# Block 0 of a fused attention and two-MLP kernel in another order: first weights fetched first, memory values copied by GpSimd, three value chunks sent from ScalarE

## The chip, the cores and the metric

The kernel runs on one core of a Trainium2 chip. The metric is the device time of one execution in microseconds (us), the median of three runs. Engines are named as in the profile: PE (TensorE matmul), PEld (its weight load), DVE (VectorE), ACT (ScalarE), POOL (GpSimd) and SP (SyncE, which here only issues DMAs).

## What is computed

Chunked attention with eight memory keys and values, then two MLPs one after the other, all in float32. The reference, cut:

```python
def _attn_ref(q, k, v, mem_k, mem_v):      # q, k, v: (4, 8, 768, 64); mem: (4, 8, 8, 64)
    for c in range(S // 32):               # chunks of 32 queries
        k_ctx = k[:, :, max(0, 32 * c - 16):min(S, 32 * c + 40)]        # v_ctx the same
        k_full, v_full = concat(mem_k, k_ctx), concat(mem_v, v_ctx)
        scores = scale * (q_c @ k_full.T)
        a = exp(scores - max(scores)); a = a / (sum(a) + 1e-09)
        out[:, :, 32 * c:32 * c + 32] = a @ v_full

def _moe_ref(x, w1, w2, w3, w_out):        # x: 3072 tokens x 512, d_ff 768
    return maximum(maximum(x @ w1, x @ w2), x @ w3) @ w_out

def _moe2_ref(x, w_in, w_out):             # d_ff 2048
    h = x @ w_in
    g = where(h >= 1, h, where(h <= -1, 0, (h + 1) ** 2 / 4))
    return g @ w_out
```

## The kernel before, in words

The 3072 tokens are worked in blocks of 512 (six blocks) and units of 128 (24 units, four to a block). A float32 product is made of three fast products: each operand is split into a high and a low part, and PE does high x high, high x low and low x high (L499, L500, L501). So every weight and every activation has to be split by ACT (high part) and DVE or GpSimd (low part) before PE may use it.

Block 0 is the start of the program: no weight is split yet and no attention is done. Its order is written out as a table of names, `PLAN`; each name is one step of one unit or weight, and every engine gets its instructions in the order of the table. Engines wait for each other by semaphores alone, so on each engine a step that waits holds up all that stands behind it in that engine's row. From the end of the table on, loops set the order, and they are the same in both kernels.

The steps, by their names in the table (the number is the unit, the weight or the slot):

- `d`: four matmuls on the identity matrix whose result nobody reads (`warm`, L1011); they keep PE at work.
- `lk`, `lq`: fetch a unit's keys or queries (256 KB, from SP). `lmem`, `mem`: fetch and transpose the memory keys (copied out of PSUM on DVE at L1002). `lm`: fetch the memory values of a batch (`mv`, 16 KB).
- `lv`: fetch a unit's values into its window buffer (`vw`, `vxh` or `vxl`): four chunks of 32 queries, two DMAs each, eight DMAs from SP (L265). `mv`: spread the eight memory values into the four chunks of that buffer, two DMAs from SP (L254).
- `tk`, `ck`, `ek`, `kw`, `tq`, `cq`: transposes on PE and copies on ACT that lay out keys and queries.
- `s`: the scores, 64 small matmuls (L378). `mx` on DVE: maximum and subtraction (L392, L393). `ex` on ACT: exponential (L397). `n` on DVE: sum, 1e-9, reciprocal, multiplication (L401 to L404). `a`, `ca`: transpose the probabilities (L410) and copy them. `o`: times the values (L426). `cx` on ACT: high part of the unit's activations (L436); `dx` on DVE: their low part (L440).
- `f`: fetch one weight (512 KB, L121 or L119); two weights make a pair, which lies in one of two staging buffers (`st`). A pair is split in six steps: `wa` (absolute value, ACT L134), `wr` (tail, ACT L138), `wc` (three bit operations, DVE L142, L143, L145), `wd` (their sum, DVE L150), `wh` (high part, ACT L199), `ws` (low part, DVE L204). Pair 0 holds the first two weights of the first layer, pair 1 the third one and the first of the second layer.
- `l`: a slot of the first layer, twelve matmuls of 512 columns; l0, l1 take pair 0, l2 pair 1, l3, l4 pair 2, and so on. `lt`: copy (ACT) or maximum (DVE, L534). `lh`: split of the hidden activations. `m`: a slot of the second layer.

The first slot, l0, takes the activations of units 0 to 3 and pair 0, so it stands behind `dx3` and `ws0`. `ON_DVE` and `ON_POOL` say which copies and low parts leave their usual engine; before, nothing of block 0 is on GpSimd but four memsets and the identity matrix.

Of the kernel before, what the change touches and what calls it, by code (L numbers as in the profile page):

```python
# [41 lines left out]
mv0 mx0 lq2 tk2 mv1 ck2 ek2 lk4 tq1 ex0 lv0 cq1 n0 tk3 kw1 ck3 s1 ek3 a0 kw2 mx1 tq2 lq3 tk4 cq2 f0
ck4 f1 s2 ex1 lk5 f2 d3 ek4 mx2 f3 kw3 lq4 lv2 ca0 n1 tq3 ex2 o0 cq3 n2 a1 cx0 s3 ca1 dx0 wa0 mx3 o1
wr0 tk5 wc0 a2 cx1 d7 d7 ca2 d7 ex3 d7 dx1 ck5 d7 d7 ek5 wd0 kw4 n3 wa1 tq4 f4 cq4 lv3 wc1 wr1 s4
wh0 o2 kw5 wd1 a3 d7 cx2 d7 ws0 f5 wh1 d7 lq5 f6 dx2 ca3 f7 mx4 lk7 o3 lv4 ws1 ex4 d7 cx3 d7 n4 wa2
tq5 wr2 dx3 a4 wc2 cq5 ca4 s5 l0 wa3 wd2 wr3 mx5 f9 l1 f8 wh2 lv5 wc3 ex5 lt0 o4 n5 l2 cx4 lt1 ws2
lq7 a5 lq6 wd3 ca5 l3 lm1 wa4 dx4 lk6 f11 lt2 wr4 f10 wc4 l4 lh2 lt3 wh3 wd4 tq7 o5 cq7 ws3 f13 wh4
f12 tk6 mv6 l5 cx5 ws4 lk8 ck6 lv6 dx5 wa5 lt4 tq6 lt5 wr5 m0 wc5 cq6 lh5 wa6 l6 wd5 wr6 wc6 lq8 f14
wh5 f15 tk7 l7 lt6 lk9 ck7 ws5 ek7 kw6 wd6 l8 lt7 f16 wh6 f17 ws6 s6 lt8 wa7 m1 mx6 wr7 wc7 lh8 ex6
tq8 l9 cq8 wa8 wd7 m2 wr8 wc8 f18 f19 lt9 wh7 l10 wd8 ws7 f21 wh8 f20 n6 tk8 l11 ck8 ek8 lt10 kw7  # L50
# [9 lines left out]
-  # L60
# [1129 lines left out]
```

## Time and profile before

| | |
|---|---|
| median of 3 runs | 963.79 us (961.11 to 964.07) |
| profiled execution | 960.31 us |
| its span, first to last instruction | 958.5 us |
| mean granted TensorE clock | 0.996 |
| PE busy | 938.7 us (98%) |
| DVE busy | 704.6 us (74%) |
| ACT busy | 541.9 us (57%) |
| GpSimd busy | 339.6 us (35%) |

Durations come from the profiled execution, which was 3.5 us faster than the median. The share of a whole span hides its stages, so the views that matter here are those cut to the first 125 us: the table of busy time by stretch, the timelines of single engines, and the waits.

### The profile page before, as it was taken

What the parts mean: (1) busy time and instruction counts of PE and PEld (TensorE: products, weight loads), DVE (VectorE), ACT (ScalarE), POOL (GpSimd) and SP (SyncE); (2) the same over time, 40 slices, a digit from 0 to 9 for tenths busy, and PEclk for the clock granted to TensorE, in tenths of its full rate; (3) what the DMA queues carried; (4) which work ended last, traced back from release to release, by engine and by line L of the source; (5) the groups of instructions that cost most, each with busy time, mean ns of one, the idle gap of its engine ahead of it and who ended that gap; (6) DMA issues with size and microseconds to landing.
All of it is one profiled execution on the core that took longest, in us unless ns stands there. A gap on an engine that the chain in (4) does not pass through costs nothing.

```text
span 958.5 us, 18892 instructions
## 1 busy us (share of the span) xinstructions
PE 938.7 (98%) x7090; PEld 772.4 (81%) x7090; DVE 704.6 (74%) x1001; ACT 541.9 (57%) x972; POOL 339.6 (35%) x330
## 2 busy tenths in 40 slices
PE   6799999999999999999999999999999999999998
PEld 5588887888888888888888888888888888888886
DVE  3999857687877777753337778997777988777855
ACT  5767554333343324223447777776777776777763
POOL 0000003221321111111746555555565555655642
PEclk8999999999999999999999999999999999999999
DMA  7896635676657677343414229524326744232823
GB/s 180 233 228 204 181 111 158 167 214 198 198 157 202 170 190 238 107 136 110 134 58 136 80 81 306 168 34 110 93 84 199 221 119 95 88 94 85 261 66 67
DMA packets 245900, 142.81 MB, mean 149 GB/s; under 512 B 174513, under 2 KB 223537, under 8 KB 245809
## 3 DMA queue, kind: packets, MB, share of 16 engines
q1 hardware_dynamic: 245808, 141.60, 51.9%
q8 instruction: 56, 0.92, 0.4%
q14 instruction: 36, 0.29, 0.1%
HBM read 109.71 MB, written 31.46 MB: 147 GB/s over the span
## 4 chain that ended last, share of the span: by engine, by line
PE 93%; DVE 4%; SPq 1%; DMA 1%; ACT 1%; issue 0%; POOL 0%; DVEq 0%; POOLq 0%
PE psums L499 29%; PE psums L501 29%; PE psums L500 29%; PE psums L426 2%; PE psums L378 2%; PE psums L410 1%; DMA kq<-in_k_dram 1%; PE psums L273 1%; DVE c L150 0%; PE psums L1011 0%; DVE p L404 0%; DVE p L393 0%; DVE few L392 0%; PE psums L304 0%; SPq L360 0%
## 5 line engine op out<-in xcount | busy, mean ns | idle before, releaser
L518 POOL TENSOR_TENSOR hl_a<-t,hh_a 128x512 fp32r<-128x512 f32 x30 | 41.5, 1383 | 384.6 <-ACT hh_a L516 384.6
L499 PE MATMUL psums<-xh,hi 128*128 128x512 f32 x432 | 172.2, 399 | 0.0
L501 PE MATMUL psums<-xh,lo 128*128 128x512 f32 x432 | 168.7, 390 | 0.0
L500 PE MATMUL psums<-xl,hi 128*128 128x512 f32 x432 | 168.2, 389 | 0.2 <-DVE xl L440 0.2
L810 POOL TENSOR_TENSOR hb<-h,hb 128x512 fp32r<-128x512 f32 x72 | 99.8, 1386 | 92.2 <-PE psums L501 59.5
L802 ACT CAST hb<-h 128x512 fp32r<-128x512 f32 x144 | 88.8, 622 | 48.1 <-PE psums L500 45.9
L534 DVE TENSOR_TENSOR t<-psums,t 128x512 f32<-128x512 f32 x72 | 49.4, 686 | 66.7 <-PE psums L501 66.7
L629 POOL TENSOR_TENSOR hb<-ra,hb 128x256 fp32r<-128x256 f32 x96 | 75.2, 796 | 58.8 <-ACT hb L628 53.8
L501 PEld LDWEIGHTS psums<-xh,lo 128*128 128x128 f32 x432 | 81.1, 188 | 17.8 <-DVE lo L204 0.3
L499 PEld LDWEIGHTS psums<-xh,hi 128*128 128x128 f32 x432 | 81.1, 188 | 16.5
L500 PEld LDWEIGHTS psums<-xl,hi 128*128 128x128 f32 x432 | 81.2, 188 | 16.4 <-DVE xl L440 0.6
L694 ACT ACTIVATE psums<-h 128x512 f32<-128x512 f32 x96 | 57.9, 603 | 60.0 <-DVE h L780 23.6
L501 PE MATMUL psums<-t,hb 128*128 128x512 f32 x192 | 74.8, 390 | 0.0
L499 PE MATMUL psums<-t,hb 128*128 128x512 f32 x192 | 74.7, 389 | 0.0
L500 PE MATMUL psums<-t,hb 128*128 128x512 f32 x192 | 74.7, 389 | 0.0
L629 POOL TENSOR_TENSOR hb<-rb,hb 128x256 fp32r<-128x256 f32 x72 | 55.5, 778 | 39.5 <-ACT hb L628 39.5
L808 DVE TENSOR_TENSOR hb<-psums,hb 128x512 fp32r<-128x512 f32 x66 | 44.9, 680 | 24.8 <-PE psums L501 20.3
L695 ACT ACTIVATE psums<-psums 128x512 f32<-128x512 f32 x96 | 55.9, 582 | 3.1
L499 PE MATMUL psums<-hh_a,hi 128*128 128x512 f32 x144 | 57.5, 399 | 0.0
L835 DVE TENSOR_TENSOR h<-h,h 128x1024 f32<-128x1024 f32 (+1 forms) x42 | 56.5, 1367 | 0.0
L501 PE MATMUL psums<-hh_a,lo 128*128 128x512 f32 x144 | 56.2, 390 | 0.0
L500 PE MATMUL psums<-hl_a,hi 128*128 128x512 f32 x144 | 56.2, 390 | 0.0
(145 smaller groups left out, 2235.9 us busy)
## 6 DMA issues: line engine op xcount, KB each, us to landing
ra<-cd SPq DMA_DIRECT2D x24, 512.0 KB
st<-in_moe_w_out_dram SPq DMA_DIRECT2D x22, 512.0 KB
t<-sd SPq DMA_DIRECT2D x21, 512.0 KB
st<-in_moe_w_dram SPq DMA_DIRECT2D x18, 512.0 KB
vw<-in_v_dram SPq DMA_DIRECT2D x152, 56.0 KB
st<-in_moe_w_in_dram SPq DMA_DIRECT2D x16, 512.0 KB
sd<-st SPq DMA_DIRECT2D x8, 896.0 KB
h<-yd SPq DMA_DIRECT2D x12, 512.0 KB
```

What stands on the lines that cost most here:

```text
L499: nc.tensor.matmul(out, whi, xhi, start=first, stop=False)
L500: nc.tensor.matmul(out, whi, xlo, start=False, stop=False)
L501: nc.tensor.matmul(out, wlo, xhi, start=False, stop=last)
L518: e.tensor_tensor(out=lo, in0=h, in1=hi.bitcast(F32), op=ALU.subtract)
L534: nc.vector.tensor_tensor(out=cur["t", j, f], in0=s, in1=cur["t", j, f], op=ALU.max)
L629: nc.gpsimd.tensor_tensor(out=c[:, 1], in0=t, in1=c[:, 0].bitcast(F32), op=ALU.subtract)
L694: nc.scalar.activation(out=a, in_=x, func=AF.Relu, bias=0.5, scale=0.5)
L695: nc.scalar.activation(out=a, in_=a, func=AF.Square)
L802: nc.scalar.copy(out=hi, in_=x)
L808: nc.vector.tensor_tensor(out=lo, in0=y, in1=hi.bitcast(F32), op=ALU.subtract)
L810: nc.gpsimd.tensor_tensor(out=lo, in0=x, in1=hi.bitcast(F32), op=ALU.subtract)
L835: nc.vector.tensor_tensor(out=x, in0=y, in1=z, op=op)
```

## The change

`PLAN` is another order of the same steps: the same slots, units and weights, and the same split of each weight. Three kinds of steps are new. `vs` and `vc` are one chunk of a unit's values, two DMAs each, sent from SP and from ACT (number = 4 x unit + chunk); they take the place of `lv0` to `lv7`, and three chunks, 6, 10 and 18, go through ACT. `mv0` to `mv2` are on GpSimd: two copies of 8 partitions x 1024 words each in the place of two DMAs. `mv6` stays a DMA. There are 16 `d` steps ahead of l0 where there were 18, and two more behind the last slot, m5. Of the table, the diff shows the first and the last line:

```diff
 PLAN = """
-d3 lk1 d3 lmem0 d3 d3 lk0 d3 lm0 lq0 lv1 tk1 mem0 ck1 tk0 ck0 ek1 tq0 lk2 kw0 d3 mv2 cq0 lq1 lk3 s0
...
-lq9 l16 lt15 wd11 m4 n7 wh11 ws11 a7 lt16 l17 ca7 o7 lt17 lh17 s8 cx7 dx7 m5 mx8 ex8 f24 f25 f26 f27
+d7 f0 d7 d7 d3 f1 lmem0 d7 d3 lk0 wa0 d3 lk1 wr0 tk0 wc0 ck0 tk1 wd0 mem0 ck1 ek1 d7 f3 d3 wh0 d7
...
+d7 d7 f24 f25 f26 f27
 """.split()
...
 ON_POOL = """
--
+mv0 mv1 mv2
 """.split()
 
 
@@ -248,21 +250,33 @@
                     out=mvs[b][e * 64:e * 64 + NM],
                     in_=mem_v[b].rearrange("(e h) m d -> e m h d", e=2)[e])
 
+    def load_vs(x):
+        load_v(x // NC, (x % NC,))
+
+    def load_vc(x):
+        load_v(x // NC, (x % NC,), nc.scalar)
+
     def fill_mv(u):
         mv = mvs[u // UPB]
+        if f"mv{u}" in ON_POOL:
+            for e in range(2):
+                nc.gpsimd.tensor_copy(
+                    out=vws[u][e * 64:e * 64 + NM].rearrange("p c h d -> p c (h d)"),
+                    in_=mv[e * 64:e * 64 + NM].rearrange("p (o g) d -> p o (g d)", o=1).to_broadcast([NM, NC, 4 * D]))
+            return
         for e in range(2):
             nc.sync.dma_start(
                 out=vws[u][e * 64:e * 64 + NM],
                 in_=mv[e * 64:e * 64 + NM].rearrange("p (o g) d -> p o (g d)", o=1).to_broadcast([NM, NC, 4 * D]))
 
-    def load_v(u):
+    def load_v(u, chunks=range(NC), queue=nc.sync):
         b, s0 = divmod(u, UPB)
-        for c in range(NC):
+        for c in chunks:
             t0 = s0 * P + c * CH - LEFT
             lo, hi = max(t0, 0), min(t0 + WIN, S)
             for e in range(2):
                 p0 = e * 64 + NM + lo - t0
-                nc.sync.dma_start(
+                queue.dma_start(
                     out=vws[u][p0:p0 + hi - lo, c],
                     in_=v[b].rearrange("(e h) t d -> e t h d", e=2)[e, lo:hi])
 
@@ -440,7 +454,7 @@
         nc.vector.tensor_tensor(out=lo, in0=t, in1=hi.bitcast(F32), op=ALU.subtract)
 
     parts = {
-        "lk": load_k, "lq": load_q, "lv": load_v, "lm": load_mv, "mv": fill_mv,
+        "vs": load_vs, "vc": load_vc, "lk": load_k, "lq": load_q, "lv": load_v, "lm": load_mv, "mv": fill_mv,
         "tk": st_k, "ck": cp_k, "ek": edge_k, "kw": fill_kw,
         "tq": st_q, "cq": cp_q,
         "s": st_s, "mx": st_m, "ex": st_e, "n": st_n, "a": st_a, "ca": cp_a, "o": st_o, "cx": cp_x, "dx": cp_xl,
@@ -484,7 +498,7 @@
         if kind in ("gk", "gq"):
             if i < NU // (3 if kind == "gk" else 2):
                 parts[kind](i)
-        elif kind in WEIGHTS or i < NU:
+        elif kind in WEIGHTS or i < (NU * NC if kind in ("vs", "vc") else NU):
             parts[kind](i)
 
     todo = [s for u in range(UB, NU) for s in steps(u)]
```

In the built program DVE's row began with the memory keys and the first unit's softmax:

```order
L992 MEMSET vw 32x256
L993 MEMSET vw 32x256
L1002 COPY memkT<-psums 64x32 x8
L384 MEMSET psums 32x2x4x16
L392 TENSOR_REDUCE few<-psums 128x8
L393 TENSOR_TENSOR p_215<-psums,few 128x512
L401 TENSOR_REDUCE few<-p_215 128x8
L402 TENSOR_SCALAR few<-few 128x8
L403 RECIPROCAL few<-few 128x8
L404 TENSOR_TENSOR p_215<-p_215,few 128x512
```

and now begins with pair 0 (c_136) and pair 1 (c_189), around the memory keys, ahead of the first unit's softmax:

```order
L1006 MEMSET vw 32x256
L1007 MEMSET vw 32x256
L144 TENSOR_SCALAR c_136<-c_136 128x1024
L145 TENSOR_SCALAR c_136<-c_136 128x1024
L147 SCALAR_TENSOR_TENSOR c_136<-st_110,c_136 128x1024
L152 ISA c_136<-st_110,c_136 128x2048
L1016 COPY memkT<-psums 64x32 x8
L206 TENSOR_TENSOR lo_181<-c_136,hi_180 128x1024
L144 TENSOR_SCALAR c_189<-c_189 128x1024
L145 TENSOR_SCALAR c_189<-c_189 128x1024
L147 SCALAR_TENSOR_TENSOR c_189<-st_174,c_189 128x1024
L398 MEMSET psums 32x2x4x16
```

Eight instructions moved to the front: all five of pair 0's and the three bit operations of pair 1. `few` and `p` are the first unit's softmax.

SP's row, the order of the fetches, began with k and memory keys, and reached the first weight behind five k (`kq<-in_k`), four q, the values of units 0 and 1 and the spread memory values:

```order
L233 DMA kq<-in_k_dram 128x8x64
L981 DMA memk<-in_mem_k_dram 128x2x64 x2
L233 DMA kq<-in_k_dram 128x8x64
L247 DMA mv_130<-in_mem_v_dram 8x4x64 x2
L239 DMA kq<-in_q_dram 128x8x64
L265 DMA vxh<-in_v_dram 56x4x64 x8
L233 DMA kq<-in_k_dram 128x8x64
L254 DMA vxl<-mv_130 8x4x256 x2
L239 DMA kq<-in_q_dram 128x8x64
L233 DMA kq<-in_k_dram 128x8x64
```

and now has the first two pairs (st_110, st_174) around the first k and the memory keys; no `mv` is spread by DMA:

```order
L123 DMA st_110<-in_moe_w_dram 128x4x256 x2
L995 DMA memk<-in_mem_k_dram 128x2x64 x2
L235 DMA kq<-in_k_dram 128x8x64 x2
L121 DMA st_174<-in_moe_w_out_dram 128x1024
L123 DMA st_174<-in_moe_w_dram 128x4x256
L241 DMA kq<-in_q_dram 128x8x64
L235 DMA kq<-in_k_dram 128x8x64
L249 DMA mv_202<-in_mem_v_dram 8x4x64 x2
L235 DMA kq<-in_k_dram 128x8x64
L241 DMA kq<-in_q_dram 128x8x64
L123 DMA st_267<-in_moe_w_dram 128x4x256 x2
L241 DMA kq<-in_q_dram 128x8x64
```

GpSimd's row goes, in the program's first part, from its memsets (kT) straight to block 1's work before:

```order
masks.py:199 AFFINE_SELECT ident<-ident 128x128
L986 MEMSET kT_82 128x4x16
L987 MEMSET kT_82 128x4x8
L518 TENSOR_TENSOR hl_a_0_1786<-t_0_1621,hh_a_0_1785 128x512
L169 TENSOR_TENSOR st_1603<-st_1603 128x512
```

and has the six copies between them now:

```order
masks.py:199 AFFINE_SELECT ident<-ident 128x128
L1000 MEMSET kT_82 128x4x16
L1001 MEMSET kT_82 128x4x8
L263 COPY vxh<-mv_202 8x1024 x2
L263 COPY vw<-mv_202 8x1024 x2
L263 COPY vxl<-mv_202 8x1024 x2
L532 TENSOR_TENSOR hl_a_0_1786<-t_0_1621,hh_a_0_1785 128x512
```

They take the place of the six DMAs from `mv` to the same three buffers in SP's row.

## Rows read from the trace of the kernel before

**Rows 1.** Stretch, length, busy PE, PEld, DVE, ACT, POOL, clock, DMA share, GB/s.

```profile
0.00:6.60 6.60, 5.24 (x25) 4.06 (x26) 0.54 (x2) 1.28 (x1) 0.85 (x8) 1.00 0.68 153
6.60:20.00 13.40, 7.98 (x162) 6.16 (x161) 5.54 (x17) 7.78 (x17) 0.00 (x0) 0.75 0.79 170
20.00:30.00 10.00, 7.65 (x282) 6.30 (x281) 7.58 (x16) 8.12 (x14) 0.00 (x0) 0.99 1.05 298
30.00:46.90 16.90, 11.39 (x319) 9.31 (x317) 16.38 (x24) 13.63 (x20) 0.00 (x0) 1.00 0.76 199
46.90:124.90 78.00, 78.00 (x784) 63.60 (x776) 71.36 (x93) 48.83 (x67) 0.00 (x0) 1.00 0.73 199
```

**Rows 2.** Timeline of PE, four places: start, us, line, operation, tiles, shape.

```profile
42.24 1.05 PE L1011 MATMUL psums<-ident 128*128 128x256 bf16 x8
...
46.93 0.50 PE L499 MATMUL psums<-xh,hi 128*128 128x512 f32 x1
...
56.56 0.60 PE L410 MATMUL psums<-ident,p 128*128 128x128 f32 x4
56.91 0.47 PE L499 MATMUL psums<-xh,hi 128*128 128x512 f32 x1
...
125.16 0.39 PE L499 MATMUL psums<-xh,hi 128*128 128x512 f32 x1
```

**Rows 3.** Waits of DVE up to 47 us: us in total, times, longest.

```profile
DVE few L392 <- PE psums L378: 5.0, 2, 3.1
```

**Rows 4.** Timeline of DVE from 33 to 46 us.

```profile
33.53 0.68 DVE L401 TENSOR_REDUCE few<-p 128x8 f32<-128x512 f32 x1
...
34.69 0.69 DVE L404 TENSOR_TENSOR p<-p,few 128x512 f32<-128x512 f32 x1
35.30 0.69 DVE L142 TENSOR_SCALAR c<-c 128x1024 f32<-128x1024 f32 x1
...
38.11 1.23 DVE L150 CUSTOM_DVE_ANT_0 c<-st,c 128x2048 uint16<-128x2048 uint16 x1
39.25 1.22 DVE L204 TENSOR_TENSOR lo<-c,hi 128x1024 fp32r<-128x1024 f32 x1
40.39 0.68 DVE L440 TENSOR_TENSOR xl<-psums,xh 128x512 fp32r<-128x512 f32 x1
40.99 0.68 DVE L392 TENSOR_REDUCE few<-psums 128x8 f32<-128x512 f32 x1
...
45.21 0.68 DVE L440 TENSOR_TENSOR xl<-psums,xh 128x512 fp32r<-128x512 f32 x1
```

**Rows 5.** Timeline of ACT: the first operation on a weight.

```profile
27.08 1.13 ACT L134 ACTIVATE c<-st 128x1024 f32<-128x1024 f32 x1 [0.27 <-DMA st<-in_moe_w_dram]
```

**Rows 6.** Timeline of SP's issues; DMA rate in 40 slices of 0 to 50 us.

```profile
25.57 7.39 SPq L265 DMA_DIRECT2D vxl<-in_v_dram  x8
...
GB/s 0 74 243 217 205 188 139 131 171 163 267 157 163 215 163 131 122 306 343 321 285 346 370 290 190 110 34 63 299 204 179 65 95 340 276 273 394 303 195 136
```

**Rows 7.** Timeline of GpSimd and DVE together in block 1, 146 to 149 us.

```profile
146.35 1.29 POOL L169 TENSOR_TENSOR st<-st 128x512 fp32r<-128x512 f32 x1 [1.93 <-ACT st L168]
...
146.60 0.68 DVE L401 TENSOR_REDUCE few<-p 128x8 f32<-128x512 f32 x1
...
147.60 1.29 POOL L169 TENSOR_TENSOR c<-c,st 128x512 fp32r<-128x512 f32 x1
...
147.94 1.50 DVE L404 TENSOR_TENSOR p<-p,few 128x512 f32<-128x512 f32 x1
```

**Rows 8.** GpSimd by line: ns min/median/max; by group: busy us, mean ns.

```profile
L518 POOL TENSOR_TENSOR hl_a<-t,hh_a x30: 1284/1302/1745, 142.8 to 494.5; 128x512 fp32r<-128x512 f32 x30
...
L629 POOL TENSOR_TENSOR hb<-ra,hb x96: 731/741/1720, 475.3 to 876.7; 128x256 fp32r<-128x256 f32 x96
...
masks.py:197 POOL MEMSET ident<- 128x128 f32 x1 | 0.2, 205 | 0.3 <-POOLq L1174 0.3
...
L987 POOL MEMSET kT<- 128x32 f32 x1 | 0.1, 126 | 0.0
```

More of the change, by code (lines that the diff above doesn't have):

```diff
@@ L40 @@
 PLAN = """
-d3 lk1 d3 lmem0 d3 d3 lk0 d3 lm0 lq0 lv1 tk1 mem0 ck1 tk0 ck0 ek1 tq0 lk2 kw0 d3 mv2 cq0 lq1 lk3 s0
[L42 to L50, printed above, removed]
@@ L51 @@
-ws8 wa9 tk9 lt11 l12 wr9 wc9 ck9 wa10 a6 lh11 wd9 l13 ek9 wr10 f22 f23 wc10 ca6 lt12 m3 wh9 wd10 o6
-ws9 wh10 s7 lt13 cx6 lv7 ws10 wa11 l14 mx7 wr11 kw8 dx6 l15 lq10 lt14 ex7 lk10 wc11 lk11 lh14 lm2
-lq9 l16 lt15 wd11 m4 n7 wh11 ws11 a7 lt16 l17 ca7 o7 lt17 lh17 s8 cx7 dx7 m5 mx8 ex8 f24 f25 f26 f27
+d7 f0 d7 d7 d3 f1 lmem0 d7 d3 lk0 wa0 d3 lk1 wr0 tk0 wc0 ck0 tk1 wd0 mem0 ck1 ek1 d7 f3 d3 wh0 d7
+ws0 f2 wa1 wc1 lq0 d7 kw0 lk2 lm0 d7 tq0 cq0 tk2 wr1 ck2 s0 lk3 ek2 kw1 mv1 lq1 mx0 tk3 f5 f4 lq2
@@ new lines @@
+tq1 vs2 ex0 cq1 vs3 lk4 ck3 s1 d3 ek3 vs1 wd1 n0 kw2 a0 wa2 tq2 mx1 d3 vs0 wr2 vc6 ex1 wc2 cq2 tk4
+mv0 n1 ca0 s2 o0 lq3 ck4 ek4 mv2 vs7 tq3 vs9 mx2 kw3 cx0 lk5 a1 vs4 vs5 lq4 wd2 vs8 cq3 ca1 ex2 s3
+tk5 vs11 vs14 dx0 mx3 wh2 vs13 lq5 vc10 n2 o1 d3 cx1 ex3 ck5 vs12 tq4 a2 ca2 vs15 dx1 f7 o2 vs19 ek5
+n3 kw4 cq4 cx2 f6 ws2 a3 s4 ca3 kw5 dx2 tq5 o3 mx4 cq5 cx3 dx3 s5 wh1 mx5 d7 f8 l0 ex4 ws1 wr3 n4
+wa3 wc3 vc18 f9 vs17 lt0 lk6 vs16 wd3 lq7 l1 lq6 wa4 wr4 lt1 l2 wc4 a4 tq7 ca4 cq7 wh3 o4 wd4 wh4
@@ new lines @@
+ws3 cx4 l3 tq6 ex5 f11 lt3 f10 lt2 tk6 wa5 ws4 vs22 vs21 ck6 n5 l4 a5 wc5 ca5 lk7 vs20 f13 lt4 cq6
+dx4 f12 l5 lh2 tk7 wr5 vs23 wr6 wd5 lt5 wa6 l6 wc6 ck7 wd6 wh5 l7 lt6 o5 lk8 lt7 ek7 kw6 tk8 ws5 lh5
+wh6 f14 lm1 cx5 f15 f16 wa7 mv6 ck8 s6 ws6 f17 vs27 dx5 ek8 mx6 vs25 l8 vs26 lm2 wc7 wr7 l9 kw7 lq8
+lk10 m0 lt8 vs24 ex6 wd7 lk9 f18 l10 wr8 wa8 f19 wh7 lt9 wc8 tk9 ck9 wd8 f21 wh8 ws7 m1 n6 wa9 tq8
+ws8 lt10 wr9 f20 wc9 lh8 lq10 a6 l11 ca6 wd9 l12 f22 lt11 cq8 o6 ek9 wa10 s7 wr10 cx6 vs30 f23 wc10
@@ L54 @@
+wd10 lt12 m2 l13 wh9 wh10 ws9 lq9 ws10 mx7 ex7 l14 vs29 lt13 n7 wa11 lt14 dx6 l15 wc11 kw8 wr11 wd11
+lk11 a7 vs31 l16 ca7 lh11 s8 vs28 wh11 ws11 mx8 lt15 lh14 o7 lt16 cx7 l17 lt17 dx7 m3 m4 ex8 lh17 m5
+d7 d7 f24 f25 f26 f27
 """.split()
```

## The prediction

> **What bounds the kernel now.** The page's first part comes first: PE is busy for 98% of the span and DVE for 74%, so over the whole program PE is the bound, and a change to block 0 can only take away time in which PE has no useful matmul. The table by stretch says where that is [rows 1]. From 46.9 to 124.9 us, PE is busy in 78.00 of 78.00 us; before 46.9 it is busy in 5.24 + 7.98 + 7.65 + 11.39 = 32.3 us, warming matmuls included. So the one thing to win is an earlier first slot of the first layer (l0). In the PE timeline l0 starts at 46.93, and the first slot of block 1 at 125.16: 78.2 us for block 0 behind l0 [rows 2]. From there on both kernels have the same program.
>
> What sets l0 is read from DVE's column [rows 1]: 16.38 of 16.9 us from 30 to 46.9, and 7.58 of 10 before. l0 wants the low parts of the activations of units 0 to 3 and the low weights of pair 0, and both end on DVE: the last of the four L440 starts at 45.21 [rows 4]. DVE's idle time lies at the front: up to 30 us it works for 0.54 + 5.54 + 7.58 = 13.7 us and idles for 16.3 us. The waits view names the scores on PE, 5.0 us in two waits [rows 3]; the rest is waiting for PE's first transposes and for ACT's exponentials. DVE has nothing else to do then, since the first weights are only fetched at about 20 us, and ACT starts on them at 27.08 [rows 5].
>
> **The change, step by step.** The weights of pair 0 are now fetched by the first two DMAs, and DVE's row begins with their five instructions. The arithmetic of block 0 stays: the same number of instructions of each kind on PE, ACT and DVE, dummies and DMA issues aside. What moves is DVE's start and its idle time.
>
> Start of DVE. Two fetches make 1.05 MB. In the first 50 us the DMA row shows nothing in the first slice of 1.25 us, little in the second, and up to 394 GB/s in later ones [rows 6]; at 298 GB/s (20 to 30 us, DMA share 1.05) [rows 1] from about 1.9 us they have landed at 5.4. ACT's absolute value takes 1.13 us [rows 5], so DVE starts at 6.6. Bounds: landed at 4.6 with the best slice's 394 GB/s, at 6.2 with the third slice's 243; so 0.8 us either way.
>
> DVE's work up to l0, by starts in a stretch almost without waits [rows 4]: a weight's bits (L142 to the next L150) 2.7, its sum (L150) 1.14, its low part (L204) 1.14, softmax's end (L401 to the next L142) 1.77, an activation's low part (L440) 0.60, maximum and subtraction twice 0.68. In the new order there stand ahead of the fourth L440 three weights' bits (8.1), three sums (3.4), two low parts (2.3), the memory keys' copies (1.0), five maxima (6.8), four softmax ends (7.1) and four activations (2.4): 31.1 us, if nothing waits. The old order has one pair's bits and sum less there and one softmax end more, and waits for 16 us.
>
> Does it wait? The second pair, k, q and the memory keys stand behind 1.05 MB. Pair 1 has landed after 2.75 MB: 1.9 + 9.2 + 0.6 (from last packet to signal, my guess from the few tenths by which packets precede their readers) = 11.7, its absolute value ends at 12.8. DVE has worked on pair 0 and the keys until 12.6, so 0.2 is lost. The third unit's k, which now stands ahead of the first scores on PE, has landed after 3.28 MB, at 13.5: scores at 15, and DVE is by then in pair 1's bits until 15.5. From there on every DVE step has one pair of weights standing between it and the attention chain, and I find no wait that outlasts this. So without anything else l0 would come at 6.6 + 31.1 + 0.2 = 37.9 us.
>
> GpSimd's copies. Three DMA pairs from SP are replaced by six GpSimd copies, 8 partitions by 1024 words each. No row of before has such a copy. Nearest is GpSimd's 128x512 subtraction, which reads 1024 words: 1.30 us in the median; the same with 256 goes in 0.74 [rows 8]. If it is the written words that cost, 1024 of them take 0.18 + 4 x 0.56 = 2.4 us; if only writing costs, as in the two memsets (0.126 for 32 words, 0.205 for 128) [rows 8], 0.1 + 1024 x 0.00082 = 0.94. I take 1.30. GpSimd has nothing else to do, so its own time is free, but it holds up DVE: a DVE multiplication with both operands in SBUF that starts at 147.94 under a GpSimd subtraction of 147.60 to 148.89 takes 1.50 us [rows 7] instead of 0.69 [rows 4], and ends 0.6 after GpSimd's does. A reduction beside one keeps its 0.68 [rows 7]. The memory values land right behind the third k, at about 13.8, so that the copies meet DVE's run of weights: copy 1 holds up pair 1's third bit operation (1.3 lost), copy 2 runs beside maximum and subtraction, which read PSUM (0), copy 3 goes ahead of pair 1's sum (1.2), copy 4 starts beside the softmax reduction of 0.7 (0.6), copy 5 holds up its multiplication (1.0), copy 6 runs beside the next maximum (0). Together 4.1 us; walked in the same way, 2.4 with copies of 0.94 and 10.8 with copies of 2.4. All of DVE's work ahead of l0 stands behind them, so l0 moves with it: 37.9 + 4.1 = 42.0.
>
> [...]
>
> Three chunks from ACT. Two issues each; SP's cost 7.39/8 = 0.92 us in a busy stretch [rows 6]. Four of them, up to 3.7 us of ACT, lie ahead of l0. Queued behind them on ACT are exponentials 1 and 3 and one activation's high part, for which DVE waits; but ACT, 30.8 us busy in the first 46.9 [rows 1], is given 4 us of air by the copies that delay DVE. I take 0, and 1 us if DVE is not delayed. SP gains the six issues and the three pairs.
>
> Behind l0. PE now has one transposition more there (a4, 0.35, the distance from 56.56 to 56.91) and two warming groups after the block's last slot, where PE is not waiting: eight matmuls, 1.05 [rows 2]. So 1.4 us come back. DVE must keep up: behind l0 it is busy in 71.36 of 78 us [rows 1], which leaves room. Going through the new order with the same prices, each low weight is ready before its slot, by 0 us (l8) to 13 (l3); the last pair by about 1 us. So no new stall, 0.5 us at most.
>
> The sum: 46.9 - 42.0 - 1.4 = 3.5 us. The profiled execution took 960.31 us, span 958.5; its span would become 955.0. The median of the runs, 963.79, lies 3.5 above that execution; I take the difference from the median: 960.3.
>
> **The rivals.**
> Cheap copies: they are shorter than 1.3 us, or they give way to DVE, or fall into waits of DVE that I don't see. Then 46.9 - 38.9 (with 1 us for ACT's issues) - 1.4 = 6.6 us are won: 957.2. For it: the copies touch 8 partitions only, and they are the one term without a row of its own. Against: the multiplication at 147.94 was held up to the end of GpSimd's instruction.
> [...]
> Slower: the copies take what the 128x512 subtraction's written words say, 2.4 us each. DVE then loses 10.8 us ahead of l0, which comes at 48.7: 46.9 - 48.7 - 1.4 = -3.2, 967.0. It decides from about 1.9 us for a copy on, where the loss passes 7.6.
>
> **How the numbers follow.** Forecast 0.50, its own range with copies of 0.94 to 1.6 us and DVE's start 0.8 either way, not both at their worst: 958.2 to 962.1. Cheap copies 0.20, clock or late data 0.17, slower 0.13. About 0.3% (2.9 us) is what a measurement of this kernel can tell. Faster by more: 0.7 of the forecast's 0.50, and cheap copies, 0.55. Within: 0.15 of the forecast and the 0.17, 0.32. Slower: 0.13. The range leaves out most of the slower case and the best tenth: 956.5 to 965.5.
>
> **What would show it.** Right: DVE's first weight operation at 6 to 7.4 us; six copies on GpSimd between 13 and 25 us, and beside them multiplications and bit operations of DVE of 1.2 us and more; l0 at 41 to 43; PE without idle time to the end of block 0; a first slot of block 1 at about 121.7. Copies of less than 1 us, or DVE's operations at 0.69 beside them, show the cheap case (l0 at 39); copies of 2 us and more the slow one; a granted clock under 1 behind l0 the clock's. Wrong altogether would be a DVE that waits for scores between 15 and 38 us, or slots that wait for low weights.

## The result and the profile after

| | before | after |
|---|---|---|
| median | 963.34 us (961.11 to 964.07, 4 runs) | 971.95 us (969.09 to 973.27, 4 runs) |
| profiled execution, its span | 960.31 us, 958.5 | 969.09 us, 967.3 |
| first slot of block 0 (l0) | 46.93 | 50.31 |
| first slot of block 1 | 125.16 | 133.86 |
| from there to the end of the span | 833.3 | 833.4 |

The change makes the kernel slower: ratio 1.0089, 95% interval 1.0061 to 1.0118. (The row of before is from the measurement beside the changed kernel.) The time lies above the range. The last row says where to look: behind block 0 both kernels take the same time (in the profiled executions of the fifteen experiments it is 833.3 to 834.0), so the whole loss of 8.7 us lies in block 0, 3.4 ahead of l0 and 5.3 behind it. Places like l0 are those of one profiled execution, and single executions of one kernel differ by some 3 to 4 us (961.11 to 964.07 before, 969.09 to 973.27 after; the profiled one of the change is its fastest), so a difference of 1 us at l0 between two kernels is not shown by one trace each.

The table by stretch, after; columns as in [rows 1]:

```profile
0.00:6.60 6.60, 4.58 (x28) 3.36 (x28) 0.54 (x2) 0.54 (x1) 0.85 (x8) 1.00 0.75 211
6.60:20.00 13.40, 8.20 (x110) 6.29 (x110) 10.93 (x17) 10.75 (x17) 5.29 (x4) 0.87 1.19 280
20.00:30.00 10.00, 7.35 (x209) 6.03 (x209) 9.55 (x16) 7.99 (x15) 3.63 (x3) 0.66 0.69 134
30.00:46.90 16.90, 10.48 (x391) 8.54 (x384) 13.06 (x21) 11.12 (x21) 0.00 (x0) 1.00 0.66 157
46.90:124.90 78.00, 72.62 (x788) 59.51 (x788) 69.07 (x91) 48.32 (x69) 0.00 (x0) 0.98 0.77 203
```

DVE has what the change is made for: 10.93 us of work from 6.6 to 20 where it had 5.54, and 9.55 instead of 7.58 in the next stretch. It gives part of it back from 30 to 46.9 (13.06, before 16.38), and PE is no longer full from 46.9 on (72.62 of 78).

The timeline of PE, after; the bracket is the idle time ahead and what ended it:

```profile
34.03 0.90 PE L440 MATMUL psums<-aT,vxh 64*64 64x32 f32 x48 [0.26 <-issue]
36.27 0.43 PE L440 MATMUL psums<-aT,vxh 64*64 64x32 f32 x16 [1.34 <-issue]
...
41.23 0.45 PE L392 MATMUL psums<-kw,qTb 64*32 64x64 f32 x30
42.88 0.51 PE L392 MATMUL psums<-kw,qTb 64*32 64x64 f32 x34 [1.20 <-issue]
...
45.27 0.43 PE L392 MATMUL psums<-kw,qTb 64*32 64x64 f32 x25
48.80 0.89 PE L392 MATMUL psums<-kw,qTb 64*32 64x64 f32 x39 [3.10 <-issue]
...
50.31 0.78 PE L513 MATMUL psums<-xh,hi 128*128 128x512 f32 x1
50.88 0.63 PE L514 MATMUL psums<-xl,hi 128*128 128x512 f32 x1
51.31 0.63 PE L515 MATMUL psums<-xh,lo 128*128 128x512 f32 x1
...
117.78 0.86 PE L392 MATMUL psums<-kw,qTb 64*32 64x64 f32 x64
120.95 1.14 PE L440 MATMUL psums<-aT,vw 64*64 64x32 f32 x64 [2.31 <-DVE p L407]
```

Three things stand there. First, PE stops three times in the middle of a step, o1, s4 and s5, though a step's 64 matmuls wait for nothing within it: 48 + 16, 30 + 34 and 25 + 39, and no releaser but "issue" (the engine waited for nothing that the profile shows). Counted in the trace, where a matmul is two instructions, its weight load and itself, the three places are PE's instructions 961, 1217 and 1473, 256 apart. Records of 16 KB "instruction" transfers (fetches of instructions) start at 33.84, 40.47 and 46.15, each 2.4 to 2.7 us ahead of PE's going on. The reading is that PE has no instructions there; in all seventeen traces every stop of over 0.3 us with the releaser "issue" in the first 60 us stands at one of the counts 705, 961, 1217 and 1473, give or take one or two, whatever step that is. Second, l0's first matmuls are 0.57 and 0.43 us apart instead of 0.23: the lower clock level (granted clock 0.51 from 48.5 to 52), from the end of the stop of 3.1 us on. Third, at 118.64 to 120.95 o7 waits for mx8 (L407). The kernel before has only one such stop, of 1.3 us, also at instruction 961, and there it falls into warming matmuls:

```profile
32.55 1.81 PE L1011 MATMUL psums<-ident 128*128 128x256 bf16 x15 [1.29 <-issue]
```

Its next two fetches start at 33.95 and 37.98 and end 2.1 and 7.1 us before they are needed.

The timeline of DVE, after:

```profile
8.54 0.69 DVE L144 TENSOR_SCALAR c<-c 128x1024 f32<-128x1024 f32 x1 [7.04 <-ACT c L136]
...
14.84 1.53 DVE L144 TENSOR_SCALAR c<-c 128x1024 f32<-128x1024 f32 x1
16.40 1.42 DVE L145 TENSOR_SCALAR c<-c 128x1024 uint32<-128x1024 uint32 x1
17.85 1.93 DVE L147 SCALAR_TENSOR_TENSOR c<-st,c 128x1024 uint32<-128x1024 uint32 x1
...
21.34 1.51 DVE L152 CUSTOM_DVE_ANT_0 c<-st,c 128x2048 uint16<-128x2048 uint16 x1
...
37.90 0.69 DVE L454 TENSOR_TENSOR xl<-psums,xh 128x512 fp32r<-128x512 f32 x1 [0.70 <-ACT xh L450]
...
43.47 0.69 DVE L406 TENSOR_REDUCE few<-psums 128x8 f32<-128x512 f32 x1 [1.31 <-PE psums L392]
...
46.05 0.69 DVE L454 TENSOR_TENSOR xl<-psums,xh 128x512 fp32r<-128x512 f32 x1 [1.17 <-ACT xh L450]
49.78 0.11 DVE L400 MEMSET psums<- 32x64 f32 x1 [3.04 <-PE psums L392]
```

The start at 8.54, four operations that GpSimd holds up, and the waits at 37.90, 43.47 and 46.05: they come from o1, s4 and o3, which PE has late by its stops. The fourth activation's low part (dx3) starts at 46.05; s5, cut in two by the stop of 3.10, and a warming group behind it keep l0 back 3.7 us more. GpSimd's timeline, after:

```profile
14.54 2.73 POOL L263 COPY vxh<-mv 8x1024 f32<-8x1024 f32 x2 [13.08 <-DMA mv<-in_mem_v_dram]
17.32 3.36 POOL L263 COPY vw<-mv 8x1024 f32<-8x1024 f32 x2
20.74 3.01 POOL L263 COPY vxl<-mv 8x1024 f32<-8x1024 f32 x2
```

The six copies take 9.1 us with hardly a gap, beside the held operations above. ACT's timeline, after:

```profile
6.06 1.28 ACT L136 ACT_TABLE_LOAD   x1 [6.06 <-DMA st<-in_moe_w_dram]
7.36 1.15 ACT L136 ACTIVATE c<-st 128x1024 f32<-128x1024 f32 x1
```

The load of ACT's function table lies between the weights' landing and the first work on them.

### The profile page after: what moved, and what is told of

Read it like the earlier page. It is cut to its first block, busy times and chain, and to the rows that moved or that the text cites. A ratio compares the mean times of both kernels' runs of the same rounds, so it can differ in the third digit from the quotient of the medians.

```text
span 967.3 us, 18886 instructions
## 1 busy us (share of the span) xinstructions
PE 940.6 (97%) x7090; PEld 773.9 (80%) x7090; DVE 709.1 (73%) x1001; ACT 540.9 (56%) x972; POOL 348.2 (36%) x336
## 4 chain that ended last, share of the span: by engine, by line
PE 90%; DVE 4%; DMA 3%; SPq 1%; issue 1%; ACT 1%; ACTq 0%; DVEq 0%
PE psums L513 28%; PE psums L515 28%; PE psums L514 28%; PE psums L440 2%; PE psums L392 2%; DMA st<-in_moe_w_dram 2%; PE psums L424 1%; DVE c L152 0%; DVE c L147 0%; DMA kq<-in_q_dram 0%; DMA kq<-in_k_dram 0%; PE psums L287 0%; SPq L374 0%; DVE p L407 0%; DVE few L406 0%
```

## The experiments

Ratios are against the kernel before, measured beside each variant; l0 and block 1 are their first slots in the profiled execution. Line numbers of variants shift by a few.

### Parts of the change one by one

**The copies alone, on the kernel before** (`fill_mv` as in the change, the table as before), in two measurements:

```diff
 ON_POOL = """
--
+mv0 mv1 mv2
```

> The kernel before with one part of the change alone: mv0, mv1 and mv2 as six GpSimd copies instead of six transfers, the table as it was. Theory A (copies are not where the loss comes from; they hold DVE for about 3 us at most where DVE has 5 us of waits to give, and take six issues off SP): 961 to 964, ratio 0.998 to 1.002. [...]

> The kernel before with the six copies on GpSimd alone, once more in five rounds beside the other two. If its gain is real: ratio 0.9965 to 0.999, the interval below 1. If the first result was a chance of that chip: 0.999 to 1.001.

Measured: 959.96 us, ratio 0.9977 (0.9963 to 0.9991), and 960.22 us, 0.9981 (0.9968 to 0.9993). Faster by some 2 us, small but twice with the interval below 1, and below the 961 to 964 us written down for the first measurement; this version is faster than both kernels. What brings the gain is not shown. The copies lie where DVE mostly waits or reads PSUM (5.81 to 12.31 us), and there the pair takes 2.12 us, 1.06 a copy. GpSimd's timeline in this kernel, and behind it DVE's:

```profile
5.81 2.12 POOL L255 COPY vxl<-mv 8x1024 f32<-8x1024 f32 x2 [4.35 <-DMA mv<-in_mem_v_dram]
7.99 2.14 POOL L255 COPY vw<-mv 8x1024 f32<-8x1024 f32 x2
10.18 2.13 POOL L255 COPY vxh<-mv 8x1024 f32<-8x1024 f32 x2
```

```profile
10.76 0.17 DVE L390 MEMSET psums<- 32x128 f32 x1 [3.49 <-PE psums L384]
```

**The changed kernel without the copies** (six DMAs again):

```diff
 ON_POOL = """
-mv0 mv1 mv2
+-
```

> The changed kernel with the memory values spread by SP's DMAs again, all else as changed. Theory of the copies (GpSimd's copies cost DVE about 3 us early, and that 3 us reaches the first slot): DVE's bit operations and sum of pair 1 go back from 1.53, 1.42, 1.93 and 1.51 us to 0.69, 0.69, 1.23 and 1.22; the first slot comes at 47 to 48 instead of 50.3; the time falls by 2 to 3 us, to about 969. Theory of the instruction stream (the first slot is late because PE runs out of instructions ahead of it): DVE is 3 us faster, but PE still stands still for over 1 us after every 256 of its instructions, and the first slot gains 0 to 3 us; the stalls of 1.3, 1.2 and 3.1 us just before it stay. If the copies were the whole loss, the kernel would be back at 963.

Measured: 973.63 us, ratio 1.0114 (1.0088 to 1.0140), l0 at 52.96. DVE's operations are back at 0.69 and 1.23, but PE waits 4.9 us for keys, and one stop of 1.39 in s5 stays; l0 is later than either theory had it. So copies in place of DMAs are not the loss; the interval overlaps that of the change, and what the copies take from DVE they give back to the transfers.

**The first weights alone, on the kernel before:**

```diff
-d3 lk1 d3 lmem0 d3 d3 lk0 d3 lm0 lq0 ...
+f0 f1 d3 lk1 d3 lmem0 d3 d3 lk0 wa0 wr0 wc0 wd0 d3 lm0 lq0 ...
```

(and f0, f1, wa0, wr0, wc0 and wd0 taken out of their old places)

> The kernel before with one other part alone: f0 and f1 (first weights) at the head of the table, and wa0, wr0, wc0, wd0 right behind lk0; all else in the old order. Theory A (an early start of the weights is worth little in itself: attention's data come about 4 us later, ScalarE's table load waits behind the weights, and TensorE reaches dense steps later): 962 to 969, ratio 1.000 to 1.007, first slot at 45 to 50. Rival D (the early weights do bring the gain of 3 to 5 us forecast, and only the rest of the new order spoils it): 957 to 960, first slot at 42 to 44.

Measured: 963.40 us, ratio 1.0002 (0.9988 to 1.0016), l0 at 50.32, block 1 78.0 us behind it. The theory that early weights by themselves bring 3 to 5 us falls. DVE has them at 8.38, waits later 3.0 for the first scores, 2.7 for later ones, and PE stops 1.34 us inside s5.

**The three chunks from SP instead of ACT:**

```diff
-... vs0 wr2 vc6 ex1 ... lq5 vc10 n2 ... wa3 wc3 vc18 f9 ...
+... vs0 wr2 vs6 ex1 ... lq5 vs10 n2 ... wa3 wc3 vs18 f9 ...
```

> The changed kernel with the three chunks vc6, vc10 and vc18 sent from SP like the other chunks, at the same place in the table. Theory A (ScalarE's six issues cost nothing, as forecast): 970 to 973. Rival H (they hold ScalarE, and the steps behind it, by up to 1 us): 969 to 970.5. The other way round, if SP's six more issues delay later transfers: 973 to 975.

Measured: 973.24 us, ratio 1.0121 (1.0097 to 1.0144), overlapping the change's own. No sign that ACT's issues cost anything.

### The table of functions

**A small activation ahead of the first weight:**

```diff
         make_identity(nc, ident)
+        nc.scalar.activation(out=few[:, 0, :], in_=ident[:, 0:1], func=AF.Abs)
```

> The changed kernel with one small ScalarE instruction (an absolute value of 128 words) ahead of the first weight's, so that the activation table is loaded before the weights have landed. If the load behind the wait costs what it takes (1.28 us ahead of DVE's first weight operation), DVE starts at 7.3 instead of 8.5 and the time falls by up to 1.3 us, to 970.7. If the attention chain, not DVE, sets the early stage, DVE starts earlier and the first slot stays at 50.3.

Measured: 969.90 us, ratio 1.0069 (1.0054 to 1.0084), l0 at 49.40. ACT of this kernel:

```profile
0.74 1.28 ACT L999 ACT_TABLE_LOAD   x1 [0.74 <-PEq L1189]
...
6.07 1.12 ACT L136 ACTIVATE c<-st 128x1024 f32<-128x1024 f32 x1 [3.84 <-DMA st<-in_moe_w_dram]
```

The load no longer stands behind the weights' transfer; DVE starts at 7.23 instead of 8.54, and l0 comes 0.9 earlier. The median is 2.05 lower, with intervals that overlap, and block 1 of the profiled execution starts at 135.00, later than the change's 133.86: l0's matmuls are 0.43 us apart instead of 0.23 from 49.97 to 53.38. So DVE's earlier start is shown, a gain in the total is not. Three stops in PE stay (1.78, 1.75 and 2.98).

### o7 and mx8

**o7 ahead of mx8 in the table; PE's own order stays:**

```diff
-lk11 a7 vs31 l16 ca7 lh11 s8 vs28 wh11 ws11 mx8 lt15 lh14 o7 lt16 cx7 l17 lt17 dx7 m3 m4 ex8 lh17 m5
+lk11 a7 vs31 l16 ca7 lh11 s8 vs28 wh11 ws11 o7 mx8 lt15 lh14 lt16 cx7 l17 lt17 dx7 m3 m4 ex8 lh17 m5
```

> The changed kernel with the step o7 (unit 7's values) written ahead of mx8 (unit 8's maximum) in the table, as it was before; PE's order is the same. Theory: the 2.3 us for which PE waits at 118.6 us are o7's wait for mx8, which stands behind the last weights on DVE and reads the same two banks of PSUM; written the other way round the wait is gone and the time falls by 1.5 to 2.3 us, to about 970. Rival: PE waited there for the values' DMA, and nothing changes.

Measured: 967.35 us, ratio 1.0050 (1.0036 to 1.0064). The scores of a unit and the output of another lie in two halves of the same two PSUM banks; where the table has mx8 first, o7 waits until mx8 has read, though neither uses the other's values. The stop of 2.31 is gone. PE of this kernel:

```profile
118.05 0.86 PE L392 MATMUL psums<-kw,qTb 64*32 64x64 f32 x64
118.84 1.14 PE L440 MATMUL psums<-aT,vw 64*64 64x32 f32 x64
```

The span is 2.1 shorter than the change's (965.2), which is the wait; the median moves by 4.6, more than the wait, with intervals that just overlap (1.0036 to 1.0064, 1.0061 to 1.0118). The traces show what else the wait can cost. Of the nine traced kernels that have it, seven have a stretch of some 3.4 us in which the matmuls of the slots are 0.43 us apart instead of 0.23, from 0.6 to 1.8 us behind its end on, and none of the three without it has one (x3_o7_first, x8_mended, x13_all). PE of the kernel with the small activation (x2_table), one of the seven:

```profile
120.50 1.14 PE L440 MATMUL psums<-aT,vw 64*64 64x32 f32 x64 [2.31 <-DVE p L407]
121.56 0.65 PE L513 MATMUL psums<-xh,hi 128*128 128x512 f32 x1
122.01 0.63 PE L514 MATMUL psums<-xl,hi 128*128 128x512 f32 x1
```

There eight matmuls of the slots are 0.42 to 0.45 us apart instead of 0.23, from 121.56 to 125.00, the spacing of the change's first slot at a granted clock of 0.51; as an estimate from these figures (8 x 0.20) that costs 1.6 us more. The change's own profiled execution, its fastest, is one of the two without it, so that the 5.3 us found behind l0 there leave it out.

### PE's stops: why the instructions are late

**Values of units 3 to 5 not loaded**, to empty the transfers:

```diff
         b, s0 = divmod(u, UPB)
+        if u in (3, 4, 5):
+            return
         for c in chunks:
```

> The changed kernel without the loads of the values of units 3, 4 and 5 (24 DMAs of 56 KB left out; older values are used in their place). It tells what delays PE's instruction fetches of 16 KB, which begin 3.3 to 4.2 us after the last one was used up, where PE stands still at 36.3, 42.9 and 48.8 us. If it is the kernel's own DMA traffic, the fetches begin earlier and the three stalls (5.6 us together) fall under 2 us; the first slot comes at 46 or before. If the stream has a pace of its own, the stalls stay, each over 1 us.

Measured: one execution, 970.58 us, l0 at 52.13. Against what was expected the stops were 1.34 and 5.04 us. But the stretch had not become quiet: SP, freed of the values, sent f6 to f9 (2 MB) at 37.8 to 39.4, and the next fetch of instructions started only at 44.07, with a DMA share of 0.87 to 1.07 all the while.

**The same, and f6 to f9 written behind l0 in the table:**

```diff
-... dx1 f7 o2 ... cq4 cx2 f6 ws2 ... mx5 d7 f8 l0 ex4 ws1 wr3 n4 wa3 wc3 vc18 f9 ...
+... dx1 o2 ... cq4 cx2 ws2 ... mx5 d7 l0 f7 f6 ex4 ws1 wr3 n4 wa3 wc3 vc18 f8 f9 ...
```

> The changed kernel without the transfers that crowd the stretch ahead of the first slot: the values of units 3, 4 and 5 are not loaded at all (that part of the result is left out), and f6 to f9 (2 MB of weights) are fetched behind the first slot. Theory F (the fetch of the next block of instructions waits behind the kernel's own transfers): with DMA share under 0.4 between 36 and 46 us each fetch starts within 2 us of the end of the stand-still before, as the kernel before has it (1.4 us), and the stand-stills at 41.7 and 45.7 are under 0.5 us each. Rival G (the fetch starts a fixed number of instructions ahead of need, whatever the transfers do): they stay at 1 us or more. The total says nothing here, since the later weights wait.

Measured: one execution, 972.30 us, l0 at 51.42. Its condition was not met: SP does not wait for l0 and sent the four weights at 38.5 to 41. So this run decides nothing between the two theories, but it shows the case with busy transfers once more. PE's timeline, and behind it the stretch (columns as in [rows 1]):

```profile
44.07 0.51 PE L394 MATMUL psums<-kw,qTb 64*32 64x64 f32 x34 [2.57 <-issue]
49.91 0.89 PE L394 MATMUL psums<-kw,qTb 64*32 64x64 f32 x39 [2.68 <-issue]
```

```profile
42.00:44.00 2.00, 0.00 (x0) 0.00 (x0) 0.00 (x0) 0.00 (x0) 0.00 (x0) 1.00 0.97 293
```

**The same, with f6 to f9 replaced by fills on GpSimd:**

```diff
+        if 6 <= n < 10:
+            if q not in staged:
+                staged[q] = stage.tile([P, 2, TB, 2], U32, tag="st", name=f"st{q}", bufs=2)
+            nc.gpsimd.memset(staged[q][:, i].bitcast(F32), 1.5)
+            return
```

> The changed kernel with the stretch ahead of the first slot emptied of transfers: the values of units 3, 4 and 5 are not loaded, and in place of f6 to f9 (2 MB) GpSimd fills the same tiles with a constant, so these parts of the result are left out. (In the run that wrote f6 to f9 behind the first slot, SP still sent them at 38.5 to 41 us, and the transfers were busy all through the stretch.) Theory F (the fetch of the next block of instructions waits behind the kernel's own transfers): with DMA share under 0.5 between 38 and 48 us each fetch starts within 2 us of the end of the stand-still before, and no stand-still with the releaser issue in s4 or s5 is over 0.5 us; the first slot starts at 46 to 48. Rival G (the fetch starts late whatever the transfers do, since the dense steps themselves hold it up): stand-stills of 1 us or more stay in s4 or s5, first slot at 49 or later. The total says nothing here.

Measured: one execution, 968.34 us, l0 at 46.12. PE's timeline in this kernel, and behind it two stretches:

```profile
41.17 1.17 PE L399 MATMUL psums<-kw,qTb 64*32 64x64 f32 x64
...
44.96 0.86 PE L399 MATMUL psums<-kw,qTb 64*32 64x64 f32 x64
46.12 0.47 PE L520 MATMUL psums<-xh,hi 128*128 128x512 f32 x1
```

```profile
42.00:44.00 2.00, 2.00 (x57) 1.50 (x42) 1.41 (x3) 1.51 (x2) 0.00 (x0) 0.50 0.03 9
46.00:48.00 2.00, 2.00 (x12) 1.54 (x10) 1.84 (x5) 2.00 (x3) 0.00 (x0) 1.00 0.53 104
```

s4 and s5 are whole (x64), no stop by "issue" is left up to 50 us, and the fetches start at 30.67, 35.89 and 42.31. PE's instructions and their order are those of the change, so the borders stand at the same steps; what differs is the transfers and GpSimd's fills. In the first 60 us of every trace each fetch starts about when PE passes the border one block before, or behind that, and the stop comes when it is long behind: here the three fetches start 0.95, 0.68 and 0.79 us behind that border, in the change 3.7, 4.2 and 3.3.

That the transfers are what delays them is not shown. The condition written down, a share under 0.5 from 38 to 48 us, was not met: it is 0.57, with 0.03 from 42 to 44, beside 0.78 in the change. The fetch at 35.89 came in time with a share of 1.15 in the 0.68 us before it; in the change the transfers are idle at 36 to 37 us (0.00), and the fetch still waits until 40.47. And one kernel, the one before with the copies, has its fetch 8.1 us behind the border at 1217 and a stop of 1.18 us in s5 in one of its two traces (p1_copies), 1.9 us behind it and no stop in s5 in the other (p5_copies_again). So what starts a fetch stays open, and single executions differ in it.

**More instructions in the warming steps, the same columns**, on the change:

```diff
-            for _ in range(4):
-                nc.tensor.matmul(t[:, 0:2 * P], b[:, 0:P], b, start=True, stop=True)
+            k = 2 if len(few_d) < 14 else 1
+            few_d.append(i)
+            for _ in range(4 * k):
+                nc.tensor.matmul(t[:, 0:2 * P // k], b[:, 0:P], b[:, 0:2 * P // k], start=True, stop=True)
```

> The changed kernel, where the first 14 warming steps have eight matmuls of 128 columns instead of four of 256: the same columns, 112 more TensorE instructions ahead of all dense steps, nothing else. Theory A (TensorE's instructions come in blocks of 256, and it stands still where a block is used up before the next has come): the stand-stills move back by 112 instructions in the program: by the profile of the changed kernel's counts, to the end of s3 (about 32 to 33 us), the middle of o2 (39 to 41) and the middle of o3 (44 to 46); none of over 0.5 us with the releaser issue within o1, s4 or s5. Rival E (something else that lies at those times holds TensorE, such as the transfers or another engine's use of PSUM): they stay in o1, s4 and s5 at 34.9, 41.7 and 45.7 us. Total under both: 969 to 973.

Measured: one execution, 968.64 us, l0 at 48.05. The stops left o1, s4 and s5, and the one at s3 came, but with 0.29 us only; those forecast in o2 and o3 did not come, since their fetches (35.27, 40.62) were in time, 1.8 and 0.9 us behind the border before, although the kernel's transfers are all there. Something else took the place: 2.68 us for unit 5's q, up to 44.33. What it shows: the stops hang on the count of instructions and not on the steps o1, s4 and s5; in this execution l0 is 2.3 us earlier, the time only 0.45 under the change's profiled execution.

**The same with four warming steps (32 instructions), on the kernel before with copies:** `< 4` in place of `< 14`.

> The kernel before with mv0, mv1 and mv2 as GpSimd copies (the part that gained by itself), and with the first four warming steps cut into eight matmuls of 128 columns each: 32 more TensorE instructions. Theory A: the border of instructions that fell 23 matmuls into s5 and held it for 1.40 us at 44.4 falls ahead of s5, where TensorE waits for other work anyway; the first slot starts 0.5 to 1.4 us earlier than 46.5 and the total is 958.5 to 960. Rival E (the borders have nothing to do with it, or DVE's dx3 sets the first slot): first slot at 46.2 or later, total 959.7 to 961. The other way round, if the shifted borders hold o2 or the q transposes instead and these carry on to the end: 960 to 962.

Measured: 962.14 us, ratio 0.9996 (0.9982 to 1.0010), l0 at 48.64. The stop left s5, as expected (though the same kernel without the 32 instructions lacks it too in its second trace, p5_copies_again), and the case written down for the other way round came: the border at 961 fell into the transposes of k, in a stretch with DMA share 1.13 (24 to 28 us), and cost 3.2 us. PE of this kernel:

```profile
27.45 0.33 PE L279 MATMUL psums<-ident,kq 128*128 128x128 f32 x1
30.96 0.90 PE L279 MATMUL psums<-ident,kq 128*128 128x128 f32 x3 [3.18 <-issue]
```

So with 32 warming instructions more, of the same columns, the gain of the copies is no longer seen; the intervals of the two versions overlap (0.9963 to 0.9993 without them), so the loss by them is likely, not shown.

**s5 and mx5 behind l0:**

```diff
-... cx3 dx3 s5 wh1 mx5 d7 f8 l0 ex4 ws1 wr3 n4 wa3 wc3 vc18 ...
+... cx3 dx3 wh1 d7 f8 l0 ex4 ws1 wr3 n4 wa3 wc3 s5 mx5 vc18 ...
```

> The changed kernel with s5 and mx5 (the last unit's scores and their DVE step) written behind wc3, so behind the first slot. Theory A (TensorE gets its instructions in blocks of 256 and runs dry at each border inside dense steps): the border at 1473 matmul records then falls among slots, which use up few instructions in a us; the 3.1 us stand-still ahead of the first slot goes, the first slot starts at 46.7 to 48 instead of 50.3, and no stand-still over 0.5 us appears among the slots. s5 itself (1.6 us of dense matmuls) and whatever waits for it now lies behind the first slot, so the total falls by 1 to 3 us: 969 to 971. Rival B (the first slot is late because DVE's low parts and the transfers are late, and the stand-still only fills that time): the first slot stays at 49.5 or later, with the wait put down to DVE or a DMA, and the total stays at 971 to 973.

Measured: 971.16 us, ratio 1.0084 (1.0060 to 1.0107), l0 at 47.74. The stop of 3.1 is gone and l0 2.6 earlier, as expected, but block 1 starts at 135.96 in the profiled execution: s5's matmuls, first slots with matmuls 0.43 us apart instead of 0.23 (49.05 to 51.62) and 1.6 us for a k lie behind l0 now. What is moved over l0 is paid there; the total misses the 969 to 971 of theory A and lies in the 971 to 973 that the rival had.

### All together

**Table, o7, s5 behind l0:** the three diffs above.

> The changed kernel with three repairs together: a small activation at the very start, so that ScalarE's function table is loaded before it waits for weights; o7 ahead of mx8 in the table; s5 and mx5 behind the first slot. Theory A (the loss of the change is the sum of separate stalls: table about 2 us, order of o7 and mx8 about 2.3 us, instruction border 1 to 3 us): 972 less 5.3 to 7.3 gives 964.5 to 967. Rival B (the repairs hit the same slack, and the later start of block 1 is set by the amount of work behind the first slot): not below 967.3, the time of the repair of o7 alone.

Measured: 964.59 us, ratio 1.0022 (1.0009 to 1.0035), l0 at 45.72.

**Table, o7, 112 instructions, and no warming ahead of block 1:** the diffs above, and

```diff
-d7 d7 f24 f25 f26 f27
+f24 f25 f26 f27
```

> The changed kernel with all that the runs found: function table loaded early, o7 ahead of mx8, 112 more instructions in the warming steps (the borders of the instruction blocks moved off s4 and s5), and the two warming steps ahead of block 1 left out. Theory A (separate stalls add up): 972 less 2 (table), 4.6 (o7), 2 (borders) and 1 (warming steps) gives 961 to 964. Rival B (what is repaired ahead of the first slot comes back as low clock or as waits for transfers): 965 or more.

Measured: 962.90 us, ratio 1.0006 (0.9997 to 1.0016), l0 at 46.46, block 1 at 126.86. The repairs bring the change back to the kernel before, from 1.0089 to 1.0006, some 8 us: the stalls found are the loss. How much each is worth is less sure: o7's order has the largest part of its own (1.0050), the function table's interval overlaps the change's, and the count of instructions was not timed alone beyond one execution. What the repairs do not bring is the gain. DVE's timeline in this kernel, PE's, and a stretch:

```profile
39.85 0.69 DVE L406 TENSOR_REDUCE few<-psums 128x8 f32<-128x512 f32 x1 [0.54 <-PE psums L392]
45.44 0.69 DVE L454 TENSOR_TENSOR xl<-psums,xh 128x512 fp32r<-128x512 f32 x1 [4.17 <-ACT xh L450]
```

```profile
41.75 1.12 PE L318 MATMUL psums<-ident,kq 128*128 128x128 f32 x4 [1.94 <-DMA kq<-in_q_dram]
42.80 1.93 PE L440 MATMUL psums<-aT,vw 64*64 64x32 f32 x64
```

```profile
30.00:46.00 16.00, 11.66 (x410) 9.63 (x411) 10.91 (x19) 9.22 (x16) 0.00 (x0) 0.75 0.70 171
```

DVE works from 7.34 to 39.3 with 0.2 us of waits and has only dx3 left at 41.3, as the forecast wanted. Then it waits 4.17 us: o3, from which dx3 comes, stands on PE behind the transposes of unit 5's q (tq5), which is late by 1.94, and takes 1.93 us for 64 matmuls that take 1.13 in the change, in a stretch with a granted clock of 0.75 (30 to 46).

## Why the prediction was wrong, point by point

**Where time can be won** was right: block 0 alone decides, and within it the two slots.

| step | forecast | measured |
|---|---|---|
| DVE's first weight operation | 6.6 | 8.54 |
| DVE's work ahead of dx3's end, without copies and waits | 31.1 | 32.2 (8.54 to 46.65, less the next two) |
| copies' cost on DVE | 4.1 | 2.6 (the four held operations against their other rows) |
| waits of DVE | 0.2 | 3.4 (0.19 + 0.70 + 1.31 + 1.17) |
| dx3's end to l0 | 0 | 3.7 |
| l0 | 42.0 | 50.31 |
| behind l0, against 78.2 | +1.4 | +5.3 |

**DVE's start** was 1.9 late. The weights landed at about 6.0 instead of 5.4, and ACT's load of its function table, 1.28 us, stands behind the wait for them (at 6.06); in the kernel before it lay at the front (at 0.73), under other waits, and the sum left it out.

**DVE's work** was sized rightly, within 1.1 us.

**The copies** were the term with the widest bounds and not what failed: 1.06 us alone, against 1.30 taken, 1.4 to 1.7 beside DVE in the mean of a pair, with a cost of 2.6. Both engines are held up where they meet. In this trace copies and operations end in turns: the first copy at 15.82, DVE's first operation at 16.37, the second copy at 17.27, the next operation at 17.82. So neither engine comes first each time, and at 14.84 to 19.8 three of DVE's operations take 1.4 to 1.9 us. Two that read PSUM keep their 0.69 beside a copy (at 20.01 and 20.73); the sum had 0 there.

**"I find no wait that outlasts this"** is the step that failed. The walk followed DVE's row and took PE's steps at their durations, each begun when its inputs were there. It had no place for PE without instructions: 1.34 and 1.20 us in o1 and s4, which DVE then waited for, and 3.10 in s5, right ahead of l0. They stand in the two rows of the table in which most of l0's 8.3 us was lost, 3.4 instead of 0.2 and 3.7 instead of 0. The rows of the kernel before have the same sign once, as 1.3 us with the releaser "issue" in warming matmuls, where it cost nothing; the prediction did not ask what it would cost in real work. And with the stops mended, a late q on PE's row ahead of o3 (1.94 us) and the lower clock (0.75 from 30 to 46 us) still hold dx3 to 45.44 (x13_all); neither was in the walk.

**ACT's chunks at 0**: nothing in the runs speaks against it.

**"No new stall" behind l0** failed too: o7's 2.31, 0.93 for a k (at 91.03) and 0.24 for the copy of transposed probabilities (ACT, L428) are waits; the lower clock on l0's first matmuls (0.51 from 48.5 to 52) costs 0.8 (1.77 us from 50.31 to the fifth, for four matmuls that take 0.9 when they are 0.23 apart). With the 1.15 of a4 and the warming groups (0.80 from 133.06 to 133.86) that makes 5.4, within a tenth of the 5.3 found; in most other traces with o7's wait the wider spacing behind it (0.43 us) adds to that, by the estimate above 1.6. The walk of the order asked whether low weights are ready; it did not ask which steps share a bank.

**The rivals.** The slower one had the sign, and with 967.0 some 3 of the 8.6 us, by a mechanism that the copies' 1.06 us alone and 1.4 to 1.7 beside DVE rule out; that much was luck. Of the clock or late data, at 0.17 in the chances, the clock came, on l0's first matmuls, at 0.8 us. Of the list of signs, the copies' place (14.54 to 23.75) came; DVE's start, l0, a PE without idle time and block 1's place did not. Neither of the two signs of being wrong altogether caught what happened: DVE's wait for scores came later than the 15 to 38 us written there, at 43.47, and no slot waited for low weights; o7 waited for a bank.

## What to carry to other kernels

Where an order of work is made denser, PE's instructions become a stream to be planned for: look for stops inside a step with the releaser "issue", and count the instructions between them; where such a border falls into a long run of small matmuls, 256 instructions last PE 3 to 5 us (in the change), and a fetch that starts 3 to 4 us behind the border before, takes 1 and lets PE go on 1.4 behind its end comes late. Whether quieter transfers help is not shown. A step written ahead of the one that the path needs (a transpose for the next unit ahead of this unit's output, a reading of a bank ahead of a writing of its other half) was a wait here as soon as its input was late: 1.94 us for tq5 ahead of o3 (x13_all), 2.31 us for mx8 ahead of o7 (the change). A part that gains by itself, here the copies, is best measured by itself before it goes into a new order.

## What the runs showed of the hardware

- PE stopped at places 256 instructions apart (961, 1217 and 1473 in the change) where a fetch of 16 KB came late: 1.34, 1.20 and 3.10 us in the change, up to 5.04 (x4_no_v345), with a restart 1.4 to 1.5 us behind the end of the fetch in the change. A fetch started 0.7 to 1.0 us behind PE's passing of the border before in a kernel without stops (x11_quiet) and 3.3 to 4.2 behind it in the change; what sets that time is open.
- Behind o7's wait of 2.3 to 2.5 us the matmuls of the slots were 0.43 us apart instead of 0.23 for some 3.4 us in seven of nine traces. In the change l0's first matmuls had that spacing at a granted clock of 0.51 (48.5 to 52).
- The load of ACT's function table took 1.28 us: in the change at 6.06, right ahead of the first activation and behind that activation's wait for the weights; in the kernel before at 0.73, in the change with an early activation at 0.74 (x2_table).
- Six GpSimd copies of 8 x 1024 words took 1.06 us each with DVE mostly idle or at PSUM (p1_copies) and 1.4 to 1.7 beside it, in the mean of a pair (the change); four of DVE's operations at SBUF took 1.42 to 1.93 us there instead of 0.69 and 1.23, and two that read PSUM kept their 0.69.
